# Gated mix of two attentions: maxima from half sums and half differences, branch A in two halves of positions

## The chip, the core and the metric

The kernel runs on one core of a Trainium2 chip. Its time is the device time of one launch in microseconds. Lines are cited as L274, by their number in the kernel's file; the numbers L353 to L508 with a name of the changed kernel beside them are lines of that one.

## The reference

x has 2048 positions of 512 features, everything is fp32, both branches have 32 heads of 16.

```python
g = sigmoid((x * gate_w).sum(-1, keepdims=True))
# A: every position attends to itself and the 7 positions 2, 4, .. 14 before it
qkv = (x @ wqkv) -> q, k, v per head
idx = pos[:, None] - 2 * arange(8)            # masked where < 0
a = softmax(q . k[idx] / 4) @ v[idx] @ wo_A
# B: all heads share one key and one value head, every position sees all 2048
q = (x @ wq) per head;  k = x @ wk;  v = x @ wv    # k, v: 2048 x 16
b = softmax(q k^T / 4) v @ wo_B
out = g * a + (1 - g) * b
```

Branch B alone has 32 x 2048 x 2048 scores. Each is needed twice: once for the row's maximum, once for the exponential.

## The kernel before, in words

Products of full precision are made of three: each operand is split into a rounded part and the rest (`split`; names ending in h and l), and high x high, high x low and low x high are summed.

*Units of branch B.* The queries are cut into 32 units (4 query blocks of 512 x 8 groups of 4 heads). A unit's scores are computed twice. First for the maxima: a "fill" multiplies 128 queries of a unit with 512 keys into PSUM and VectorE reduces it to one maximum per query. A unit has 64 fills, all units 2048; they are taken two at a time into the 1024 wide tile pm (`fill_pair`, L274) or singly into ps or po (`fill_one`, L285). When a unit is complete its maxima are transposed, split (`shift_a`, `shift_c`) and stored by DMA into two more rows of the unit's query tile, so that the second product comes out as score minus maximum. The second time is a "step": 16 steps a unit, 512 in all, each for 128 keys x 2048 query columns. A step is four matmuls (L316) into pe0 and pe1, two exponentials on ScalarE (ACT, L318) into pexp, and four matmuls with the values (`weighted`, L326) that accumulate in po. After a unit's 16th step VectorE transposes po, and GpSimd (POOL) multiplies with the reciprocal of the sum and the gate (L346, L347); every second unit a delayed task transposes the result into ob (`finish_c`).

*Stages.* The prologue makes keys and the first queries. The front runs "lumps" (L698): 14 query lumps (12 matmuls of 128x512; ACT copies, POOL subtracts, SyncE (SP) stores hi, hi, lo) and 64 lumps of branch A's projection (`a_project`, 12 matmuls of 128x384, or 128x402 for the first 16; L159 to L161; ACT copies them to `stage` and every second is stored to the DRAM array ad). The projection's weights come in four groups (`load_wa`, `split_wa`), a group every 16 lumps; the splits and loads are ACT's and POOL's. Between lumps `front_fills` puts fills into pm, pl2, ps and po, as these come free. Then comes the main part: the 512 steps, with the rest of the fills between them (`fill_ready`), and four out phases (`out_phase`, L756), each of which projects four outputs: `prepare` and `turn` put B's and A's result into split form, the matmuls L529 run in 64-row halves on both halves of the PE array, `out_store` adds the halves and stores.

*Branch A* runs on POOL for all 128 partitions, each with 16 consecutive positions, in 16 groups of 2 heads. Per group: `a_load` (L368; one DMA issued by POOL itself: 16 positions and the 14 before them, 96 columns), `a_scores` in two parts (8 products L381, trees of adds L386, L388), VectorE's maximum (`a_max`, L397), POOL's subtraction (L402), ACT's exponential (`a_exp`), VectorE's sum and reciprocal (`a_sum`, L411), POOL's scaling (L418, L419) and `a_values` (8 multiplies L424, 7 adds L426). aext has two buffers, lg, amx and asum two.

*Who sets the order.* Each engine runs its instructions in the order in which the program issues them (manual schedule). The program keeps an estimated clock per engine (`clk`), a time at which each PSUM tile comes free (`free`), a list of `tasks` with due times on PE's clock, and for branch A a clock of POOL (`pool`, ns). `run_pool` issues POOL's next piece of branch A once `pool` is within 3 us of PE's clock, and the other engines' share of a group as a hook with a due time: `a_max` 6000 ns after the scores, `a_exp` and `a_sum` 4000 and 6500 ns after the subtraction. None of these estimates makes an engine wait on the chip; they only fix where in its queue an instruction stands. What an instruction waits for on the chip are its operands and buffers. An out phase starts when branch A has no more pieces to issue, the units of its query block are done and the fills are ahead by less than 1.6 units (`lead`, L753 to L756). In the order that comes out the four out phases stand at steps 320, 369, 417 and 483, and 457 fills are done before the first step, 1591 remain.

Of the kernel before, what the change touches and what calls it, by code (L numbers as in the profile page):

```python
# [6 lines left out]
F32 = mybir.dt.float32  # L7
# [6 lines left out]
P = 128  # L14
# [24 lines left out]
NF = 2 * NU * 2 * 4 * 4  # L39


T_R, T_LAT, T_EXP, T_RED2, T_RED1, T_W, T_LUMP, T_Q = 0.23, 0.20, 0.92, 1.14, 0.61, 1.18, 2.53, 3.2
# [3 lines left out]
def gated_mix_kernel(ctx, tc, xt, wa, wk, wq, wo_a, wo_b, out):  # L46
# [19 lines left out]
    eb = [None, None]  # L66
# [3 lines left out]
    pl = tc.alloc_tile_pool(name="psum_front", bufs=1, space=PSUM)  # L70
    lb = [pl.tile([P, 512], F32, name=f"pl{k}") for k in range(2)]
    eb[1] = pl.tile([P, 2, 512], F32, name="pl2")
# [45 lines left out]
    def load_wa(gg):  # L118
        n = GN + (0 if gg else VN)
        waraw[gg] = p1.tile([P, C, GN + VN], F32, name="waraw", bufs=1)  # L120
        nc.gpsimd.dma_start(waraw[gg][:, :, :n], wa.rearrange("(c p) n -> p c n", p=P)[:, :, GO[gg]:GO[gg] + n])

    def split_wa(gg):
        n = GN + (0 if gg else VN)
        wah[gg] = p1.tile([P, C, GN + VN], F32R, name="wah", bufs=2)
        wal[gg] = p1.tile([P, C, GN + VN], F32R, name="wal", bufs=2)
        split(wah[gg][:, :, :n], wal[gg][:, :, :n], waraw[gg][:, :, :n], nc.gpsimd)
        return 4200
# [25 lines left out]
    nc.vector.tensor_scalar(mk[:, 4:5], mk[:, 5:6], -2.0, 1.0, op0=ALU.mult, op1=ALU.add)  # L154

    def three(out_ap, ah, al, bh, bl):
        mms = []
        for c in range(C):
            mms.append(lambda c=c: nc.tensor.matmul(out_ap, ah(c), bh(c), start=(c == 0), stop=False))  # L159
            mms.append(lambda c=c: nc.tensor.matmul(out_ap, ah(c), bl(c), start=False, stop=False))  # L160
            mms.append(lambda c=c: nc.tensor.matmul(out_ap, al(c), bh(c), start=False, stop=(c == C - 1)))  # L161
        return mms

    def keys(t):
        pk = lb[t % 2]
# [10 lines left out]
    def queries(m, bank):  # L176
        qb, cc = divmod(m, NHG // 2)
        cs = slice(cc * P, (cc + 1) * P)
        mms = three(bank, lambda c: wqh[:, c, cs], lambda c: wql[:, c, cs], lambda c: xh[:, qb, c, :], lambda c: xl[:, qb, c, :])

        def post():
            hi = p0.tile([P, 512], F32R, name="qhi", bufs=3)
            lo = p0.tile([P, 512], F32R, name="qlo", bufs=2)
            if m < 2:
                split(hi, lo, bank)
            else:
                own = p0.tile([P, 512], F32, name="qraw", bufs=1)
                nc.scalar.activation(hi, bank, AF.Copy)
                nc.scalar.activation(own, bank, AF.Copy)
                nc.gpsimd.tensor_sub(lo, own, hi.bitcast(F32))  # L190
            for s, src in enumerate((hi, hi, lo)):
                nc.sync.dma_start(qd[s, :, qb, 8 * cc:8 * cc + 8, :], src.bitcast(F32))

        return mms, post
# [3 lines left out]
    def a_project(gg, j, bank):  # L198
        n = GN + (0 if gg else VN)
        t, r = j // 4, slice(j % 4 * P, (j % 4 + 1) * P)  # L200
        mms = three(bank[:, :n], lambda c: xh[:, t, c, r], lambda c: xl[:, t, c, r], lambda c: wah[gg][:, c, :n], lambda c: wal[gg][:, c, :n])

        def post():
            if j % 2 == 0:
                stage["t"] = p1.tile([P, GC, 2, AN], F32, name="stage", bufs=2)
            nc.scalar.activation(stage["t"][:, :, j % 2, :], bank[:, :GN].rearrange("p (g n) -> p g n", g=GC), AF.Copy)  # L206
            if gg == 0:
                nc.scalar.activation(vst[:, j, 0:DH], bank[:, GN:GN + DH], AF.Copy)
                nc.scalar.activation(gate[:, 1, j:j + 1], bank[:, GN + DH:GN + DH + 1], AF.Copy)
# [628 lines left out]
```

## Time and profile before

| | us |
|---|---|
| median of 3 runs (lowest, highest) | 1558.71 (1558.28, 1558.99) |
| the profiled execution | 1558.82 |
| its span in the trace | 1557.0 |

The table of busy shares in the prediction is over the whole span: an engine at 98% can still be idle where another sets the pace in a short stretch, and an engine at 54% can be full in one stage and idle in the next. So the prediction reads it by stretches of time. The front's query lumps end at 90.1 us, its last projection starts at 311.1, the first weighted product at 315.13; branch A's loads start between 149.2 and 893.0. In a row of groups the columns are line, engine, operation, tile written <- tiles read, shapes, count, then busy us and mean ns, then the idle us of that engine ahead of these instructions and what ended most of it. In a row of the table of stretches they are the stretch, its length, busy us and count of PE, PEld (weight load), VectorE (DVE), ACT, POOL, then granted clock, DMA share and GB/s; where the row is restricted to one line only that line's columns are left. A row of waits names who waited for whom: total us, count, longest us.

### The profile page before, as it was taken

Reading aid. Unit: us, or ns where it says so; the run is one execution under the profiler, and the core shown is the slowest. Engines: PE = TensorE matmul, PEld = TensorE weight load, DVE = VectorE, ACT = ScalarE, POOL = GpSimd, SP = SyncE. Lnnn points to the kernel's source line nnn. Section 1 sums busy time; section 2 is a strip of 40 time slices with the busy share of each in tenths; the row PEclk is TensorE's granted clock in tenths of the full one; section 3 lists DMA queues with packets and bytes.
Section 4 is the critical chain, followed back from the end, with each engine's and each line's share of the span. In section 5 each row is a group of like instructions: output and inputs, shape, how many; then the busy total and the mean of one; then the engine's idle time right before and its main releaser. Section 6 shows DMA issues by size and latency. Waiting matters only on the chain.

```text
span 1557.0 us, 25703 instructions
## 1 busy us (share of the span) xinstructions
PE 1525.7 (98%) x10076; PEld 703.8 (45%) x10076; DVE 1335.8 (86%) x1667; ACT 1120.9 (72%) x1315; POOL 834.2 (54%) x1015
## 2 busy tenths in 40 slices
PE   8999999999999999999999999999999999999998
PEld 4677777733333333333333333363354336333532
DVE  6899999979888898888899889898898889888731
ACT  4223111189999899999989998939966993999676
POOL 7420897778987898889887885240031004000210
PEclk9999999999999999999999999999999999999999
DMA  7842312211011101211111010000000000000000
GB/s 240 261 141 90 120 62 91 99 59 41 21 49 49 56 19 50 65 47 34 50 49 56 20 48 12 22 28 12 12 19 21 12 2 29 2 2 1 2 1 27
DMA packets 42889, 78.61 MB, mean 50 GB/s; under 512 B 8544, under 2 KB 25024, under 8 KB 40720
## 3 DMA queue, kind: packets, MB, share of 16 engines
q1 hardware_dynamic: 20224, 35.56, 7.9%
q0 software_dynamic: 4640, 26.99, 5.0%
q10 hardware_dynamic: 17904, 14.42, 2.8%
q8 instruction: 79, 1.29, 0.3%
q14 instruction: 42, 0.34, 0.1%
HBM read 46.96 MB, written 29.45 MB: 49 GB/s over the span
## 4 chain that ended last, share of the span: by engine, by line
PE 82%; DVE 12%; ACT 4%; issue 1%; DMA 0%; DVEq 0%; POOL 0%; ACTq 0%
PE po L326 30%; PE pe L316 21%; PE pm L253 9%; PE ps L253 8%; DVE mx L274 7%; PE pe L529 5%; DVE mx L285 4%; ACT pexp L318 3%; PE pl L159 3%; PE pl L160 2%; PE pl L161 2%; PE pl L167 1%; PE pl L253 1%; DVE ml L297 0%; PE po L253 0%
## 5 line engine op out<-in xcount | busy, mean ns | idle before, releaser
L318 ACT ACTIVATE pexp<-pe 128x1024 f32<-128x1024 f32 x1022 | 989.2, 1022 | 105.2 <-PE pe L316 100.4
L274 DVE TENSOR_REDUCE mx<-pm 128x2 f32<-128x1024 f32 x610 | 743.9, 1219 | 144.3 <-PE pm L253 140.9
L326 PE MATMUL po<-pexp,vst 128*32 128x512 f32 x4088 | 545.3, 605 | 0.7 <-ACT pexp L318 0.6
L316 PE MATMUL pe<-qst,kst 64*128 64x512 f32 x2044 | 467.0, 452 | 11.1 <-ACT pexp L318 5.8
L316 PEld LDWEIGHTS pe<-qst,kst 64*128 64x128 f32 x2044 | 191.1, 184 | 518.4 <-ACT pexp L318 506.2
L285 DVE TENSOR_REDUCE mx<-ps 128x1 f32<-128x512 f32 x597 | 405.5, 679 | 0.0
L253 PE MATMUL pm<-kst,qst 62*128 62x512 f32 x1230 | 262.6, 417 | 0.8 <-DVE mx L274 0.2
L253 PE MATMUL ps<-kst,qst 62*128 62x512 f32 x597 | 242.6, 406 | 0.4
L381 POOL TENSOR_TENSOR pr<-aext 128x512 f32<-128x512 f32 x128 | 163.9, 1302 | 57.1 <-DMA aext<-ad 57.0
L326 PEld LDWEIGHTS po<-pexp,vst 128*32 128x32 f32 x4088 | 80.4, 108 | 176.4 <-issue 163.3
L206 ACT ACTIVATE stage<-pl 128x384 f32<-128x384 f32 x64 | 31.5, 492 | 165.3 <-PE pl L161 162.8
L426 POOL TENSOR_TENSOR oa<-oa,av 128x512 f32<-128x512 f32 x112 | 143.5, 1281 | 8.8
L346 POOL TENSOR_TENSOR rl<-rl,gate_t 128x16 f32<-128x16 f32 x31 | 6.8, 220 | 242.6 <-DVE rl L342 242.6
L253 PEld LDWEIGHTS pm<-kst,qst 62*128 62x128 f32 x1230 | 117.4, 186 | 41.4 <-DVE mx L274 17.2
L253 PEld LDWEIGHTS ps<-kst,qst 62*128 62x128 f32 x597 | 111.1, 186 | 30.4 <-DVE mx L285 22.3
L424 POOL TENSOR_TENSOR av<-aext,lg 128x512 f32<-128x512 f32 x112 | 118.9, 1061 | 7.5
L305 POOL DMA_DIRECT2D qst<-ml x48 | 27.3, 573 | 134.6 <-DVE ml L297 130.8
L159 PE MATMUL pl<-wah,xh 128*128 128x384 f32 (+1 forms) x256 | 93.7, 366 | 0.4 <-ACT stage L206 0.4
L274 DVE TENSOR_REDUCE mx<-pl 128x2 f32<-128x1024 f32 x75 | 91.1, 1215 | 0.0
L160 PE MATMUL pl<-wal,xh 128*128 128x384 f32 (+1 forms) x256 | 87.1, 340 | 0.0
L161 PE MATMUL pl<-wah,xl 128*128 128x384 f32 (+1 forms) x256 | 86.9, 339 | 0.0
L529 PE MATMUL pe<-woh,turned 64*128 64x512 f32 x496 | 84.3, 400 | 0.1
(124 smaller groups left out, 1204.4 us busy)
## 6 DMA issues: line engine op xcount, KB each, us to landing
aext<-ad POOLq DMA_DIRECT2D x16, 1440.0 KB, 6.2
qst<-qd SPq DMA_DIRECT2D x64, 192.0 KB
ad<-stage ACTq DMA_DIRECT2D x32, 384.0 KB
qd<-qhi SPq DMA_DIRECT2D x32, 256.0 KB
xraw<-xt SPq DMA_DIRECT2D x16, 256.0 KB
qd<-qlo SPq DMA_DIRECT2D x16, 256.0 KB
qst<-ml SPq DMA_DIRECT2D x208, 2.0 KB
out<-two SPq DMA_DIRECT2D x12, 256.0 KB
```

What stands on the lines that cost most here:

```text
L159: mms.append(lambda c=c: nc.tensor.matmul(out_ap, ah(c), bh(c), start=(c == 0), stop=False))
L160: mms.append(lambda c=c: nc.tensor.matmul(out_ap, ah(c), bl(c), start=False, stop=False))
L253: nc.tensor.matmul(dst, qst[v % NB][b:b + 62, pr, t * P:(t + 1) * P], kst[b:b + 62, kc * 512:(kc + 1) * 512], start=True, stop=True)
L274: nc.vector.tensor_reduce(m[:, :, pr, t, kc], dst, AX.X, ALU.max)
L285: nc.vector.tensor_reduce(m[:, odd, pr, t, kc:kc + 1], dst, AX.X, ALU.max)
L316: nc.tensor.matmul(bank[:, odd, :], kst[b:b + 64, kt * P:(kt + 1) * P], qst[u % NB][b:b + 64, pr, :], start=True, stop=True)
L318: nc.scalar.activation(e, bank, AF.Exp, scale=SCALE)
L326: nc.tensor.matmul(po[32 * i:32 * i + 32, :], vst[:, kt, :], pexp[s, i // 2][:, i % 2, :], start=(kt == 0), stop=(kt == NJ - 1))
L381: nc.gpsimd.tensor_mul(pr[:, k], q, e[:, o:o + NJ, AC:2 * AC])
L424: nc.gpsimd.tensor_mul(av, e[:, o:o + NJ, 2 * AC:].rearrange("p j (h d) -> p j h d", d=DH), lg[:, w].unsqueeze(3).to_broadcast([P, NJ, AG, ...
L426: nc.gpsimd.tensor_add(ao, ao, av)
L529: nc.tensor.matmul(eb[x % 2][:, b, :], st[h], mv[h], start=first, stop=last)
```

## The change

*Maxima.* For two keys the larger of two scores s1 and s2 is (s1 + s2)/2 + |s1 - s2|/2. The change computes at the first projection lump (`half_sums`, `half_parts`) half sums and half differences of paired keys, kcd: keys n and n + 512 are a pair. From then on in the front, and where PE's streams of 64-row halves run, an event takes two key blocks of 128 queries at once: `fill_diff` multiplies with the half differences into pm and ACT takes absolute values (L373 of the changed kernel, 2 x 512 wide); `fill_sum` multiplies with the half sums into ps or po, and one VectorE instruction adds the absolute value and reduces with max (L383, tensor_tensor_reduce). Two sums with their event stand for four fills. By the written order 90 events and 180 sums do 360 fills in the front; 451 fills in all are done before the first step, 1597 remain. kcd's tiles take the place of the query tiles; the copies L353 on ACT write them.

*Front in halves.* Each lump's matmuls run as two chains of 64 rows in the two halves of the PE array, beside each other and beside a fill's (`stream`), into the two halves of pe0 or pe1. The two are added after: for query lumps ACT copies, POOL adds, ACT rounds, POOL subtracts; for projection lumps ACT copies one half and VectorE adds (L245). Stores and the rest become tasks.

*Branch A in halves of positions.* Each group's 16 positions are two pieces of 8 (`hf`), first 16 groups for hf = 0, then 16 for hf = 1: 32 loads of 8 + 14 positions (1056 KB in place of 1440), each with its maximum (L499, DVE), subtraction, exponential (L508, ACT), sum and values. `a_scores` makes products of four offsets at a time. `work()` is a generator that yields after each POOL instruction, so that POOL's work stands finer between other things. Hooks are due after 4500, 2500 and 4500 ns. The weight groups are loaded and split in quarters.

*Out phases* may start once the half of branch A that they need is done: they stand at steps 268, 377, 430 and 483; `prepare` and `turn` have single buffers of their own, the next output's come later in the stream, `finish_c` is due after 7 in place of 26 us. `fill_ready`'s slack goes from 0.15 to 0.5 (pm) and 0.3 (ps).

```diff
+NH = NJ // 2
+LEAD, M2S, M1S = 1.5, 0.5, 0.3
...
-    eb = [None, None]
+    eb = [pp.tile([P, 2, 512], F32, name=f"pe{k}") for k in range(2)]
     m2 = pp.tile([P, 2, 512], F32, name="pm")
     m1 = pp.tile([P, 512], F32, name="ps")
     po = pp.tile([P, 512], F32, name="po")
 
...
+    def load_wa(gg, c):
...
+    sel = p0.tile([P, 2, P], F32R, name="sel")
+    for x in range(2):
+        nc.vector.tensor_scalar(sel[:, x].rearrange("p (b s d) -> p b s d", b=2, s=4), whole_k.unsqueeze(2).to_broadcast([P, 2, 4, DH]), 0.5 - x, 0.0, op0=ALU.mult, op1=ALU.add)
...
+    def queries_post(m, bank):
+
+        nonlocal pool
+        settle("rest", 0)
+        two = p0.tile([P, 2, 512], F32, name="two", tag="wqr", bufs=1)
+        nc.scalar.activation(two, bank, AF.Copy)
+        at = after("act", clk["pe"] + T_LAT, 0.92)
+        own = p0.tile([P, 512], F32, name="qraw", bufs=1)
+        nc.gpsimd.tensor_add(own, two[:, 0], two[:, 1])
+        pool = max(pool, 1e3 * at) + 1400
+        hi, lo = parts_of()
+
+        def rest():
+            nonlocal pool
+            nc.scalar.activation(hi, own, AF.Copy)
+            nc.gpsimd.tensor_sub(lo, own, hi.bitcast(F32))
+            pool = max(pool, 1e3 * after("act", 0, 0.6)) + 1400
+            queries_out(m, hi, lo)
...
+
+        tasks.append((pool / 1e3, rest, (), "rest"))
 
     stage = {}
...
+            settle("store", 1)
+            stage["t"] = p1.tile([P, GC, 2, AN], F32, name="stage", bufs=2)
+        st = stage["t"]
+        two = pm[0].tile([P, GN + VN], F32, name="two", bufs=1)
+        nc.scalar.activation(two[:, :n], bank[:, 1, :n], AF.Copy)
+        at = after("act", clk["pe"] + T_LAT, 0.45) + 0.1
+        free[f"e{x}"] = at + 1.5
+
+        def rest():
+            nc.vector.tensor_add(st[:, :, j % 2, :], bank[:, 0, :GN].rearrange("p (g n) -> p g n", g=GC), two[:, :GN].rearrange("p (g n) -> p g n", g=GC))
             if gg == 0:
+                nc.vector.tensor_add(vst[:, j, 0:DH], bank[:, 0, GN:GN + DH], two[:, GN:GN + DH])
+                nc.vector.tensor_add(gate[:, 1, j:j + 1], bank[:, 0, GN + DH:GN + DH + 1], two[:, GN + DH:GN + DH + 1])
+            free[f"e{x}"] = after("dve", at, 0.5 if gg else 0.75) + 0.1
             if j % 2 == 1:
                 dst = ad[gg * GC:(gg + 1) * GC, HALO:, :].rearrange("g (p j) n -> p g (j n)", j=NJ)
+                tasks.append((free[f"e{x}"], lambda: nc.scalar.dma_start(dst[:, :, (j - 1) * AN:(j + 1) * AN], st.rearrange("p g j n -> p g (j n)")), (), "store"))
+            if j == NJ - 1:
+                tasks.append((free[f"e{x}"] + 0.5, whole, (gg,)))
+
...
-    slots = [(v, pr, t, kc) for kc in range(4) for v in range(2) for pr in range(2) for t in range(4)]
+    slots = [(v, pr, t, kc) for kc in range(2) for v in range(2) for pr in range(2) for t in range(4)]
+    slots += [(v, pr, t, kc) for v in range(2) for pr in range(2) for t in range(4) for kc in range(2, 4)]
     slots += [(v, pr, t, kc) for v in range(2, NU) for pr in range(2) for t in range(4) for kc in range(4)]
...
+            if v <= NB:
+                nc.scalar.activation(mx[v].rearrange("p b i t k -> p (b i t k)"), ident[:, 0:64], AF.Identity, scale=0.0, bias=mk[:, 6:7])
...
+    def half_sums():
+
+        clk["pe"] = max(clk["pe"], free["m2"], free["m1"], free["po"]) + 2.0
+        for g in range(2):
+            for x in range(2):
+                for y in range(2):
+                    nc.tensor.matmul(hb[g][x], sel[:, x * y], kst[:, (2 * g + y) * 512:(2 * g + y + 1) * 512], start=(y == 0), stop=(y == 1))
+
+    def half_parts():
+        kcd.append(pm[0].tile([P, 2, 2, 512], F32R, name="kcd", bufs=1))
+        dd.append(pm[0].tile([P, 2, 512], F32, name="dd", bufs=1))
+        for g in range(2):
+            for x in range(2):
+                parts, src = kcd[0][:, g, x], hb[g][x]
+                nc.scalar.activation(parts, src, AF.Identity, scale=mk[:, 0:1])
+                nc.vector.scalar_tensor_tensor(parts, src, mk[:, 1:2], parts.bitcast(F32), op0=ALU.mult, op1=ALU.add)
...
+    def half_mm(dst, v, pr, t, kc, x, odd):
+        b = 64 * odd
+        nc.tensor.matmul(dst, qst[v % NB][b:b + 62, pr, t * P:(t + 1) * P], kcd[0][b:b + 62, kc // 2, x, :], start=True, stop=True)
+
+    def fill_diff():
+        v, pr, t, kc = slots.pop(0)
+        slots.pop(0)
+        for odd in range(2):
+            half_mm(m2[:, odd, :], v, pr, t, kc, 1, odd)
+        at = after("pe", 0, T_R) + T_LAT
+        for odd in range(2):
+            nc.scalar.activation(dd[0][:, odd], m2[:, odd, :], AF.Abs)
+            ready_d[odd] = after("act", at, 0.52) + 0.1
+        free["m2"] = ready_d[1]
+        pend.extend([(v, pr, t, kc, 0), (v, pr, t, kc, 1)])
+
+    def fill_sum():
+        v, pr, t, kc, odd = pend.pop(0)
+        m = unit_tile(v)
+        dst, key = ((m1, "m1"), (po, "po"))[odd]
+        half_mm(dst, v, pr, t, kc, 0, odd)
+        nc.vector.tensor_tensor_reduce(dd[0][:, odd], dst, dd[0][:, odd], 1.0, -FMAX, ALU.add, ALU.max, m[:, odd, pr, t, kc:kc + 1])
+        free[key] = after("dve", max(clk["pe"] + T_R + T_LAT, ready_d[odd]), T_TTR) + 0.08
...
-                tasks.append((at + (26.0 if pieces else 2.0), finish_c, (u, obp["t"])))
+                tasks.append((at + (7.0 if pieces else 2.0), finish_c, (u, obp["t"])))
...
-        t = wp.tile([P, HALO + NJ, AN], F32, name="aext", bufs=2)
+    def a_load(g, hf):
+        e = wp.tile([P, HALO + NH, AN], F32, name="aext", bufs=2)
         src = ad[g]
-        nc.gpsimd.dma_start(t.rearrange("p r n -> p (r n)"), bass.AP(tensor=src.tensor, offset=src.offset, ap=[[NJ * AN, P], [1, (HALO + NJ) * AN]]))
-        aext[g] = t
-
+        nc.gpsimd.dma_start(e.rearrange("p r n -> p (r n)"), bass.AP(tensor=src.tensor, offset=src.offset + NH * hf * AN, ap=[[NJ * AN, P], [1, (HALO + NH) * AN]]))
+        aext[g] = e
+
+    def a_scores(g, hf):
...
+        for w4 in range(0, W, 4):
+            pr = p2[0].tile([P, 4, NH, AC], F32, name="pr", bufs=1)
+            for k in range(4):
+                o = HALO - DIL * (w4 + k)
+                nc.gpsimd.tensor_mul(pr[:, k], q, e[:, o:o + NH, AC:2 * AC])
+                yield 700
...
+                nx = p2[0].tile([P, 4 * NH * AG, n], F32, name=f"tr{n}", bufs=1)
                 nc.gpsimd.tensor_add(nx, cur[:, :, 0:n], cur[:, :, n:2 * n])
+                yield 160 * n + 100
                 cur = nx
-            nc.gpsimd.tensor_add(lg[:, w2:w2 + 2].rearrange("p k j h -> p (k j h)"), cur[:, :, 0], cur[:, :, 1])
-        if half:
-            for w in range(1, W):
...
+    def a_values(g, hf):
...
+            av = p2[0].tile([P, NH, AG, DH], F32, name="av", bufs=1) if w else ao
+            nc.gpsimd.tensor_mul(av, e[:, o:o + NH, 2 * AC:].rearrange("p j (h d) -> p j h d", d=DH), lg[:, w].unsqueeze(3).to_broadcast([P, NH, AG, DH]))
+            yield 700
             if w:
                 nc.gpsimd.tensor_add(ao, ao, av)
-
...
     def prepare(j, n):
-        turned[j] = wp.tile([P, 2, 2, C, P], F32R, name="turned", tag="aext", bufs=2)
+        hi, lo = turned[j, 1] = [pe[0].tile([P, C, P], F32R, name=f"own{x}", bufs=1) for x in range(2)]
...
     def turn(j, n, k):
...
+        hi = pe[0].tile([P, C, P], F32R, name="turned0", bufs=1)
...
+    def stream(seq, mm, done, pooled):
+
+        at, told = [0, 0], 0
+        while min(at) < len(seq):
+            single, odd = None, -1
+            if pend:
+                if free[("m1", "po")[pend[0][4]]] <= clk["pe"] + 0.1 and ready_d[pend[0][4]] <= clk["pe"] + 0.4:
+                    single, odd = fill_sum, pend[0][4]
+            elif paired() and not half:
+                pass
+            elif fillable() and free["m1"] <= clk["pe"] + 0.1:
+                single, odd = lambda: fill_one(m1, "m1"), half[0][4] if half else 0
...
+            dur = 0.0
+            for b in (0, 1) if odd != 1 else (1, 0):
+                if b == odd:
+                    now = clk["pe"]
+                    single()
+                    clk["pe"] = now
+                elif at[b] < len(seq):
+                    dur = mm(b, seq[at[b]])
+                    at[b] += 1
+            after("pe", 0, dur or T_R)
+            if paired():
+                if not half and not pend and max(free["m2"], clk["dve"] - 0.7) <= clk["pe"] + 0.1:
+                    fill_diff()
+            elif slots and fillable() and free["m2"] <= clk["pe"] + 0.1:
+                clk["pe"] = max(clk["pe"], free["m2"])
+                fill_pair(m2, "m2")
+            while told < min(at):
+                told += 1
+                done(seq[told - 1])
...
+    def work():
+
+        def sub(g, hf):
+            yield lambda: ("max", g, hf) in done
+            a_sub(g)
+            hooks.append((pool + 2500, a_exp, g, ("exp", g, hf)))
+            hooks.append((pool + 4500, a_sum, g, ("sum", g, hf)))
+            yield 450
+
+        def values(g, hf):
+            yield lambda: ("sum", g, hf) in done and (g < 8 or p2b)
+            yield from a_values(g, hf)
+            if g == NAG - 1:
+                done.add(hf)
+
+        order = [(g, hf) for hf in range(2) for g in range(NAG)]
+        for i, (g, hf) in enumerate(order):
+            yield lambda: g // GC < ready_gg
+            a_load(g, hf)
+            yield 500 if i else 6000
+            for k, x in enumerate(a_scores(g, hf)):
+                yield x
+                if k == 8 and i:
+                    yield from sub(*order[i - 1])
+            hooks.append((pool + 4500, a_max, g, ("max", g, hf)))
+            if i:
+                yield from values(*order[i - 1])
+            if 0 <= i - 9 < len(wos):
+                yield lambda: p2b
+                for f, a in wos[i - 9]:
+                    f(*a)
+                yield 1300
...
+    pieces, blocked = [work()], []
...
+            if lump[0] == "a" and lump[1:] == (0, 0):
+                settle("rest", 0)
+                half_sums()
+                p0.release()
+                branch_a()
+                pm.append(tc.alloc_tile_pool(name="maxima", bufs=1, side="right"))
+                half_parts()
+            settle(f"post{x % 2}", 0)
+            items[x] = queries(lump[1]) if lump[0] == "q" else a_project(*lump[1:])
+            clk["pe"] = max(clk["pe"], free[f"e{x % 2}"])
+        n = 512 if lump[0] == "q" else GN + (0 if lump[1] else VN)
+        l, r = items[x][i]
+        h = slice(64 * b, 64 * b + 64)
+        nc.tensor.matmul(eb[x % 2][:, b, :n], l[h], r[h], start=(i == 0), stop=(i == 3 * C - 1))
+        return T_R if n == 512 else 0.18
+
+    def done_mm(at):
+        nonlocal pool
+        x, i = at
...
+        k, n = outs // 4, C - (outs >= NJ - 4)
+        if outs < NJ and outs // NH in done and (NHG * (k + 1) - 1 in shaped if n == C else s >= 16 * (NU - 2) + 4) and (lead < LEAD or s >= 16 * (NHG * (k + 2) + 1) - 3):
+            out_phase(list(range(outs, outs + 4)), n)
+            outs += 4
...
-                fill_ready("m2", 0.15)
+                fill_ready("m2", M2S)
             elif which == "m1":
                 ahead = 2 * (16 * (NU - 2) - 8 - s) + 11 * (NJ - 4 - outs)
                 if ahead < to_go() - NF // NU or s >= 16 * (NU - 2) - 8 and ahead + 64 < to_go():
-                    fill_ready("m1", 0.15)
+                    fill_ready("m1", M1S)
```

428 lines of the change are left out of this document (204 added, 224 removed).

## The prediction

> **What bounds the kernel now.** I read the page's busy shares first, then the table of stages, the waits, and last one engine in order of time. The shares, then two stretches (PE, PEld, DVE, ACT, POOL busy; one in the front, one in the main part):
>
> ```profile
> PE 1525.7 (98%) x10076; PEld 703.8 (45%) x10076; DVE 1335.8 (86%) x1667; ACT 1120.9 (72%) x1315; POOL 834.2 (54%) x1015
> 230.00:280.00 50.00, 49.74 (x256) 38.55 (x256) 49.83 (x65) 7.95 (x17) 40.84 (x51) 1.00 0.28 91
> 700.00:800.00 100.00, 99.75 (x688) 35.66 (x686) 89.20 (x109) 90.41 (x98) 84.81 (x106) 1.00 0.15 48
> ```
>
> In the front PE and VectorE (DVE) are both full while ACT idles: the maxima are the price. In the main part PE is full, and ACT, DVE and POOL are all at 85 to 90 in 100. POOL's share over the whole span, 54%, hides that: branch A runs only from about 150 to 980 us, and there POOL has no room. Rows of branch A's load (first and last start), of who waits for it, and of POOL around one load:
>
> ```profile
> L368 POOL DMA_DIRECT2D aext<-ad x16: 549/594/607, 149.2 to 893.0; - x16
> aext<-ad POOLq DMA_DIRECT2D x16, 1440.0 KB, 6.2
> POOL pr L381 <- DMA aext<-ad: 57.0, 12, 6.9
> 434.48 0.59 POOL L368 DMA_DIRECT2D aext<-ad  x1
> 440.81 1.29 POOL L381 TENSOR_TENSOR pr<-aext 128x512 f32<-128x512 f32 x1 [5.73 <-DMA aext<-ad]
> ```
>
> The loads follow each other every (893.0 - 149.2) / 15 = 49.6 us. POOL issues one and its next instruction needs the data, so it stands for 5.73 us. POOL's instructions come in groups (count | busy, mean ns | idle before):
>
> ```profile
> L381 POOL TENSOR_TENSOR pr<-aext 128x512 f32<-128x512 f32 x128 | 163.9, 1302 | 57.1 <-DMA aext<-ad 57.0
> L386 POOL TENSOR_TENSOR tr<-pr 128x512 f32<-128x512 f32 x64 | 81.6, 1276 | 5.0
> L386 POOL TENSOR_TENSOR tr<-tr 128x256 f32<-128x256 f32 x64 | 46.8, 731 | 5.0
> L386 POOL TENSOR_TENSOR tr<-tr 128x128 f32<-128x128 f32 x64 | 25.6, 400 | 5.0
> L388 POOL TENSOR_TENSOR lg<-tr 128x64 f32<-128x64 f32 x64 | 18.8, 293 | 5.0
> L402 POOL TENSOR_TENSOR lg<-lg,amx 128x256 f32<-128x256 f32 x16 | 11.7, 734 | 0.0
> L418 POOL TENSOR_TENSOR asum<-asum,gate 128x32 f32<-128x32 f32 x16 | 3.9, 244 | 12.0 <-DVE asum L412 12.0
> L419 POOL TENSOR_TENSOR lg<-lg,asum 128x256 f32<-128x256 f32 x16 | 11.8, 734 | 1.3
> L424 POOL TENSOR_TENSOR av<-aext,lg 128x512 f32<-128x512 f32 x112 | 118.9, 1061 | 7.5
> L426 POOL TENSOR_TENSOR oa<-oa,av 128x512 f32<-128x512 f32 x112 | 143.5, 1281 | 8.8
> L346 POOL TENSOR_TENSOR rl<-rl,gate_t 128x16 f32<-128x16 f32 x31 | 6.8, 220 | 242.6 <-DVE rl L342 242.6
> L347 POOL TENSOR_TENSOR obp<-tt,rl 128x256 f32<-128x256 f32 x31 | 19.3, 622 | 2.4
> ```
>
> One head group costs POOL 8 x 1.302 + 4 x (1.276 + 0.731 + 0.400 + 0.293) + 0.734 + 0.244 + 0.734 + 8 x 1.061 + 7 x 1.281 = 40.4 us, with 2.3 us of the small idle times, some 0.3 of memsets, and 6.3 for the load: 49.3. L346 and L347 add 0.84 per unit of 16 steps. PE's own pace is read from the exponentials, two a step:
>
> ```profile
> 687.00:987.00 300.00, 266.87 (x276) 1.00 0.13 41
> 315.13 1.06 PE L326 MATMUL po<-early,vst 128*32 128x512 f32 x8
> 1044.79 1.07 PE L326 MATMUL po<-pexp,vst 128*32 128x512 f32 x8
> ```
>
> (The first is L318 alone in that stretch.) 300 / 138 = 2.174 us a step. The order written out puts the maxima of successive head groups (L397, on DVE) 23.6 steps apart, 51.3 us. POOL needs 49.3 + 1.2 = 50.5. So POOL just keeps up, by under 1 us a group; that margin is what the change spends.
>
> **The change, part by part.** *Branch A in halves.* Each half loads 1056 KB in place of 1440, then does 8 products of 256 elements, two trees as long as now (four offsets of half the rows), 8 multiplies and 7 adds of 256. A halved row isn't half a price: 1276 to 731 ns saves 545, not 638. So a product costs 1.302 - 0.545 = 0.757, an add 0.736, a multiply 0.622 (L347 is one, by a broadcast factor), L402 and L419 0.40 each. Busy: 6.06 + 5.40 + 0.40 + 0.24 + 0.40 + 4.98 + 5.15 = 22.6; idle times 1.7, memsets 0.2, less 0.2 where products overlap: 24.3. The load's landing has no row at this size; the nearest:
>
> ```profile
> waraw<-wa POOLq DMA_DIRECT2D x3, 768.0 KB, 4.9
> ```
>
> Bounds 4.5 (6.2 by bytes) and 6.2 (no gain); between the two rows by bytes it is 5.46, but the 768 KB rows are cut finer, so 5.2. The load still stands directly ahead of the product that needs it, 32 times now. Half a group: 24.3 + 5.2 = 29.5 us, two of them 59.0 against 49.3. With L346 and L347 for 12.5 steps 0.66: 30.2.
>
> In the changed order the maxima of successive halves (L499, DVE, behind POOL's last L487) stand 12 to 13 steps apart, at steps 15, 27, 39 ... 265: 250 steps for 20 halves, 12.5 x 2.174 = 27.2 us. POOL is 3.0 us late per half, and 1.3 more in eight that split a weight. DVE then stands at L499; behind it in DVE's queue are the reductions that free pm and ps, PE can't fill those, and behind PE's fill wait the exponentials. ACT's L508 waits for POOL's subtraction likewise. The planner's slack (2.5 to 4.5 us) is spent in two halves; from there POOL sets the pace. The condition is exact: step 317 comes behind the 32nd L499.
>
> When is that? The first load waits for the 16th a-lump's store, so about 149 us as now: what 16 quicker lumps gain, the switch ahead of them costs (below). Then 32 x (landing 5.2 + scores 12.3) + 31 x 0.4 + 30 x 11.8 = 926. Other POOL work queued between, with its rows:
>
> ```profile
> L76 POOL TENSOR_TENSOR wol<-os,woh 128x512 fp32r<-128x512 f32 x8 | 10.2, 1273 | 31.8 <-ACT woh L75 31.8
> L479 POOL TENSOR_TENSOR turned<-own,turned 128x512 fp32r<-128x512 f32 x12 | 15.5, 1294 | 4.8 <-ACT own L478 4.8
> L121 POOL DMA_DIRECT2D waraw<-wa x4 | 3.2, 792 | 0.9 <-POOL wal L76 0.9
> ```
>
> Eight wol 10.2; three such 1.29 for each of the four outputs of the first out phase, now at step 268: 15.5; eight weight loads and splits of 384, 8 x (0.79 + 1.0) = 14.4; L346 and L347 19 times, 16. Sum 56. So 149 + 926 + 56 = 1131 us.
>
> *What is left at step 317.* 616 maxima and three out phases. The old kernel has 613 and three at its step 320, 1044.79: 1557.0 - 1044.8 + 3 x 2.174 = 518.7 us. Span 1131 + 518.7 = 1649.7; the profiled execution adds 1558.8 - 1557.0 = 1.8, and stands 0.1 from the median 1558.71. Forecast **1651 us**.
>
> *The front* is then hidden, but sets the rival. Rows of its lumps, of the out phase, of DVE and ACT, and of the query stretch:
>
> ```profile
> L159 PE MATMUL pl<-wah,xh x256: 332/340/455, 90.1 to 311.1; 128*128 128x384 f32 x96, 128*128 128x402 f32 x32
> 202.07 0.34 PE L159 MATMUL pl<-wah,xh 128*128 128x384 f32 x1
> 202.60 0.34 PE L159 MATMUL pl<-wah,xh 128*128 128x384 f32 x1
> 1011.08 0.49 PE L529 MATMUL pe<-woh,turned 64*128 64x512 f32 x1
> 1028.30 1.10 PE L529 MATMUL pe<-wol,turned 64*128 64x512 f32 x8
> L274 DVE TENSOR_REDUCE mx<-pm 128x2 f32<-128x1024 f32 x610 | 743.9, 1219 | 144.3 <-PE pm L253 140.9
> L285 DVE TENSOR_REDUCE mx<-ps 128x1 f32<-128x512 f32 x597 | 405.5, 679 | 0.0
> L806 DVE TENSOR_TENSOR osl<-pe,part 128x512 f32<-128x512 f32 x4 | 2.6, 686 | 0.7 <-PE pe L802 0.6
> L266 DVE STREAM_TRANSPOSE mt<-ms 128x32 f32<-128x32 f32 x32 | 6.8, 212 | 1.1
> L189 ACT ACTIVATE qraw<-pl 128x512 f32<-128x512 f32 x14 | 8.3, 594 | 5.5 <-POOL qlo L190 5.5
> L497 ACT ACTIVATE two<-pe 128x1024 f32<-128x1024 f32 x16 | 16.4, 1026 | 60.1 <-PE pe L529 60.1
> L171 ACT ACTIVATE kst<-pl,mk 128x512 fp32r<-128x512 f32 x4 | 3.1, 778 | 5.7 <-PE pl L167 5.7
> 30.00:80.00 50.00, 46.10 (x207) 31.85 (x206) 42.79 (x48) 16.26 (x28) 25.60 (x19) 0.97 0.81 240
> ```
>
> Now (311.1 - 90.1) / 63.75 = 3.47 us a lump (the last L159 starts three quarters into it), with 5.9 maxima by the order: DVE 2 x 1.219 + 2 x 0.679 = 3.8, the bound. After: 180 sums (L383) do 360 maxima, each 0.69 (L806 reads PSUM and SBUF as it does) and the reading of the accumulator, 0 to 0.21 (L266, DVE's smallest); I take 0.05, since it is one element. 180 absolute values on ACT, 0.594 each, 107 us, lie beside idle ACT. The adds of two half products (L245) are 64 x some 0.54 on DVE, in place of ACT's copies. PE: 12 rounds a lump as now, 0.177 each at 384 (three in 202.60 - 202.07), 136 in all; per four maxima one round of 0.23 (four in 1.10 with the tail) and two shared with a lump's other half, 0.29: 90 x 0.52 = 47. So PE 183 against 222.
>
> *The switch* is a new wait: kcd lies where the query tiles lay, so ACT's L353 waits for the last query lump's copy (as L497, 1.0), POOL's add 1.3, copy 0.6, split 1.3 and the landing of its store (an estimate, 2 to 6); then four parts as L171, 0.78. Behind L353 in ACT's queue are the copies that free pe0 and pe1, and PE has only the half sums and two lumps until then: 0 to 12 us idle, I take 8. Net gain 30, 10 to 45: the main part starts at 90 + 8 + 183 + 4 = 285 in place of 315.
>
> *Edits at nothing:* the query copies now go through POOL (14 x 1.3 more, in a stretch where it is 25.60 of 50 us busy); ad's store stands in ACT's queue behind L245, but is issued a lump later; the single buffers of the out phase and the planner's wider slack (0.5, 0.3) can cost PE 5 us each way, and POOL covers them; cover gone, they are the +-15 of the first rival. The main part's maxima stay: 1597 against 1591.
>
> The Trainium skill, "SBUF — State Buffer", section "The DMA setup-cost knee", says every transfer pays about 2 us that doesn't shrink with its bytes, fitted as 2 us + bytes / 436 GB/s, and advises one large transfer over several small. For 1056 KB that is an estimate of 4.5 us, and for 1440 KB 5.4 where the trace has 6.2; with 4.5 the forecast would be 22 us less, 1629.
>
> **The rivals.** *POOL isn't the pace (faster).* If the loads were hidden, a half would cost 24.3 + 0.6 + 0.7 = 25.6, under 27.2, and only the front counts: 285 + 317 x 2.174 + 35 for the out phase (now 1011.08 to 1044.79) + 518.7 + 1.8 = 1530. It decides at a landing below 1.4 us. Against: each of the 16 loads now is followed at once by its reader, and so is each of the 32. *POOL nearly keeps up.* Were halves exactly half (0.651, 0.531, 0.640) and the landing 4.5: 26.7 a half, the last L499 at 1041, 1562. Against: the 256- and 512-wide rows of L386. *The maxima don't pay.* With 0.9 a sum DVE takes 90 x (1.8 + 0.55) = 211 us in the front against PE's 183; with the first rival that gives 1558, under the forecast it is hidden.
>
> **How the numbers follow.** POOL's pace 0.80, between 1590 and 1691 (landing 6.2); nearly keeping up, 1545 to 1590, 0.09; only the front, 1515 to 1545, 0.08; slower still, where stalls of PE and POOL add, 0.03. The range 1570 to 1695 leaves out 0.18. About 0.2% (1555.6 to 1561.8) is what can be told from no change: faster 0.10, same 0.02, slower 0.88.
>
> **What would show it.** Right: waits of pr for aext near 32 x 4.6 = 147 us, loads 31 us apart and the last near 1113; DVE's L499 and ACT's L508 waiting for POOL, together near 120 us; POOL near 950 busy; out phase at step 268 near 990 us. Halves near 24.3 + 5.2 prove the sizes. Wrong: L499 without idle time, pr waiting under 2 us a load, or the first step of the main part past 320.

## The result and the profile after

The changed kernel takes 1691.95 us (median of 4 runs, 1691.37 to 1692.53) against 1558.52 us (1558.28 to 1558.99): 1.0856 times as long, 95% interval 1.0837 to 1.0875. The forecast was 1651, its range 1570 to 1695. The span of the profiled execution is 1689.6 us, 132.6 more than before. First the page's shares, then one stretch of the table of stages (PE, PEld, DVE, ACT, POOL busy, then the granted clock):

```profile
PE 1546.6 (92%) x11020; PEld 738.3 (44%) x11020; DVE 1289.7 (76%) x1950; ACT 1227.1 (73%) x1504; POOL 931.4 (55%) x1525
700.00:800.00 100.00, 90.41 (x596) 31.96 (x600) 78.08 (x100) 79.30 (x87) 78.84 (x135) 0.95 0.14 46
```

In the main part no engine is busy throughout any more: PE has fallen from 99.75 to 90.41 in that stretch, and POOL, which was to be the pace, is busy for 78.84. But POOL has no time left all the same. It stands another 14.7 us there for its own three loads, and the rest are gaps between its instructions, 0.08 us each on average; in that stretch it waits for no other engine. From its first load to its last, 978 us, it waits for other engines for 19 us. So POOL and its loads do set the pace, and the others wait for it. The waits (the second row is POOL's in the stretch from 700 to 800 us, the others are of the whole span), and the first and last starts of branch A's loads, of its maxima, and of the first step:

```profile
POOL pr L478 <- DMA aext<-ad: 159.8, 32, 6.5
POOL pr L478 <- DMA aext<-ad: 14.7, 3, 5.1
ACT lg L508 <- POOL lg L504: 96.6, 30, 5.9
DVE asum L513 <- ACT lg L508: 39.3, 23, 5.2
L467 POOL DMA_DIRECT2D aext<-ad x32: 553/593/593, 157.8 to 1135.9; - x32
L499 DVE TENSOR_REDUCE amx<-lg x32: 290/366/380, 185.3 to 1159.0; 128x16 f32<-128x128 f32 x32
L424 PE MATMUL po<-early,vst x8: 1061/1061/1061, 319.7 to 320.5; 128*32 128x512 f32 x8
```

One such wait, in order of time, POOL first, then ACT:

```profile
653.24 0.59 POOL L467 DMA_DIRECT2D aext<-ad  x1
659.12 2.85 POOL L478 TENSOR_TENSOR pr<-aext 128x256 f32<-128x256 f32 x4 [5.29 <-DMA aext<-ad]
665.61 0.46 POOL L504 TENSOR_TENSOR lg<-lg,amx 128x128 f32<-128x128 f32 x1
666.03 1.41 POOL L478 TENSOR_TENSOR pr<-aext 128x256 f32<-128x256 f32 x2
```

```profile
660.17 1.94 ACT L416 ACTIVATE pexp<-pe 128x1024 f32<-128x1024 f32 x2 [0.19 <-PE pe L414]
666.10 0.31 ACT L508 ACTIVATE lg<-lg 128x128 f32<-128x128 f32 x1 [4.00 <-POOL lg L504]
666.32 3.89 ACT L416 ACTIVATE pexp<-pe 128x1024 f32<-128x1024 f32 x4
672.20 1.94 ACT L416 ACTIVATE pexp<-pe 128x1024 f32<-128x1024 f32 x2 [1.99 <-PE pe L414]
```

POOL stands 5.29 us for the load, then does 6.5 us of scores before the subtraction L504. ACT had reached its exponential of branch A (L508) at 662.1 and waits 4.00 us for that subtraction; the step's own exponentials stand behind it in ACT's queue, and behind them PE. That happens at nearly every half.

From the starts of the first weighted product of each step the difference of 132.6 us can be split by where the time appears (rounding leaves 0.1):

| | before | after | difference |
|---|---|---|---|
| first step starts | 315.1 | 319.7 | +4.5 |
| the first three steps | 9.5 | 11.7 | +2.2 |
| 23 steps of more than 4 us, 5.8 us on average (before, 23 mean steps) | 49.4 | 133.4 | +84.0 |
| the other 481 steps, each | 2.149 | 2.204 | +26.3 |
| the four steps with an out phase | 137.3 | 152.8 | +15.5 |
| from the last step to the end | 12.0 | 12.0 | 0 |

The long steps are 12 to 13 steps apart, as the halves' hooks are.

### The profile page after: what moved, and what is told of

It reads as the page before. It is cut to its first block, busy times and chain, and to the rows that moved or that the text cites. A ratio compares the mean times of both kernels' runs of the same rounds, so it can differ in the third digit from the quotient of the medians.

```text
span 1689.6 us, 28993 instructions
## 1 busy us (share of the span) xinstructions
PE 1546.6 (92%) x11020; PEld 738.3 (44%) x11020; DVE 1289.7 (76%) x1950; ACT 1227.1 (73%) x1504; POOL 931.4 (55%) x1525
## 4 chain that ended last, share of the span: by engine, by line
PE 40%; POOL 36%; DMA 12%; ACT 5%; issue 4%; DVE 3%; SPq 0%; POOLq 0%; DVEq 0%; ACTq 0%
PE po L424 13%; DMA aext<-ad 10%; PE pe L414 10%; POOL pr L478 9%; POOL tr L484 7%; POOL oa L531 7%; POOL av L528 6%; PE pe L680 4%; PE pm L299 4%; ACT pexp L416 4%; PE ps L299 3%; PE pe L870 3%; DVE mx L320 1%; DMA qd<-qlo 1%; POOL lg L487 1%
## 5 line engine op out<-in xcount | busy, mean ns | idle before, releaser
L416 ACT ACTIVATE pexp<-pe 128x1024 f32<-128x1024 f32 x1022 | 987.2, 1022 | 134.0 <-PE pe L414 129.4
L320 DVE TENSOR_REDUCE mx<-pm 128x2 f32<-128x1024 f32 x554 | 676.5, 1221 | 208.9 <-PE pm L299 202.9
L478 POOL TENSOR_TENSOR pr<-aext 128x256 f32<-128x256 f32 x256 | 182.1, 734 | 159.9 <-DMA aext<-ad 159.8
L531 POOL TENSOR_TENSOR oa<-oa,av 128x256 f32<-128x256 f32 x224 | 164.3, 734 | 16.8
L528 POOL TENSOR_TENSOR av<-aext,lg 128x256 f32<-128x256 f32 x224 | 139.6, 623 | 14.7
L373 ACT ACTIVATE dd<-pm 128x512 f32<-128x512 f32 x180 | 98.0, 596 | 43.1 <-PE pm L364 38.9
L870 PE MATMUL pe<-wah,xh 64*128 64x384 f32 (+1 forms) x512 | 119.9, 355 | 8.3 <-DVE stage L245 6.1
L870 PE MATMUL pe<-wal,xh 64*128 64x384 f32 (+1 forms) x512 | 120.5, 348 | 0.0
L870 PE MATMUL pe<-wah,xl 64*128 64x384 f32 (+1 forms) x512 | 119.7, 346 | 0.0
L383 DVE CUSTOM_DVE_ANT_0 dd<-ps,dd 128x512 f32<-128x512 f32 x90 | 62.0, 689 | 41.9 <-PE ps L364 19.2
L484 POOL TENSOR_TENSOR tr<-pr 128x512 f32<-128x512 f32 x64 | 81.5, 1273 | 4.8
L870 PEld LDWEIGHTS pe<-wah,xh 64*128 64x128 f32 x512 | 74.7, 194 | 13.7 <-ACT dd L373 6.2
```

The costliest lines, as they stand in the source:

```text
L320: nc.vector.tensor_reduce(m[:, :, pr, t, kc], dst, AX.X, ALU.max)
L373: nc.scalar.activation(dd[0][:, odd], m2[:, odd, :], AF.Abs)
L416: nc.scalar.activation(e, bank, AF.Exp, scale=SCALE)
L478: nc.gpsimd.tensor_mul(pr[:, k], q, e[:, o:o + NH, AC:2 * AC])
L484: nc.gpsimd.tensor_add(nx, cur[:, :, 0:n], cur[:, :, n:2 * n])
L528: nc.gpsimd.tensor_mul(av, e[:, o:o + NH, 2 * AC:].rearrange("p j (h d) -> p j h d", d=DH), lg[:, w].unsqueeze(3).to_broadcast([P, NH, AG, ...
```

## The experiments

**Is it the pace of POOL, or the place that the plan gives to the others?** `work()` yields 500 ns for each load but the first, whose landing it counts (6000). Added up, the plan gives a half 24.2 us, which puts successive halves 12 to 13 steps apart, some 27 us on the chip; there a half took 31.55 us ((1135.9 - 157.8) / 31). The old plan nearly fitted: 48.8 us a group (500 + 2 x 12500 + 800 + 22500) against 49.6. So the first experiment changes this number and leaves POOL's instructions as they are:

```diff
-            yield 500 if i else 6000
+            yield 6000
```

> The changed kernel; only the planner's clock of POOL now counts 6000 ns for every load of branch A, where it counted 500 for all but the first. POOL's instructions are the same; the other engines' share of a half (L499, L508, L513) moves later in their queues, 15 to 16 steps apart in place of 12 to 13. Theory A (a half costs POOL about 30 us with its load, and ACT and VectorE were made to stand behind it): POOL still takes about 30 us a half, but nobody waits for it, so L508's wait for POOL goes from 96.6 us to under 20, steps run at 2.17 us, and the time is about 1555 us (1545 to 1580). Rival B (the new order of the front and of the out phases costs the time, POOL's lateness only follows PE): within 20 us of 1692. Rival C (TensorE's lower granted clock, 0.957, is a cause by itself): the clock stays near 0.95 and the time above 1640.

1550.63 us (1548.39 to 1551.1): 0.9949 of the kernel before, 0.9934 to 0.9964. Its waits, the starts of its loads and of the first step, and the same stretch of its stages:

```profile
POOL pr L478 <- DMA aext<-ad: 135.4, 28, 7.3
L467 POOL DMA_DIRECT2D aext<-ad x32: 551/591/593, 157.6 to 1209.1; - x32
L424 PE MATMUL po<-early,vst x8: 957/1014/1062, 299.0 to 299.9; 128*32 128x512 f32 x8
700.00:800.00 100.00, 100.00 (x700) 36.03 (x697) 90.83 (x119) 91.98 (x101) 73.19 (x123) 1.00 0.16 49
```

POOL still waits 135.4 us for its loads, and it now takes longer over branch A: the last load starts at 1209.1 in place of 1135.9. Yet the kernel is 141 us shorter, because ACT waits no more for POOL's subtraction (L508 waits once, for 0.3 us, in place of 96.6 us), PE is full, and no step after the third lasts over 4 us but those with an out phase. POOL's slowness alone is not the cost. Its slowness with ACT's and VectorE's instructions placed for a faster POOL is. The front gains too: the first step starts at 299.0, so in the changed kernel some 21 us of the front's gain were lost to the same waits (18 of them in four lumps, of 9.4, 8.1, 5.0 and 6.9 us among lumps of 2.9).

**The same from the other side, in the kernel before.** Nothing of the change, one number of the plan:

```diff
-    QK, AV = 12500, 22500
+    QK, AV = 10000, 22500
```

> The kernel before with one number changed: QK, the plan's time for half a group's scores, 10000 in place of 12500 ns, so that the plan leaves out about 5 us a group, as the changed kernel's plan does with a half's landing. POOL's instructions stay as they are. Theory A (it is the plan that ties the other engines to POOL): the maxima of successive groups stand 21.3 steps apart in place of 23.6, the 16th at step 251, where the kernel before is at 860 us and POOL's 16th group has its scores near 925: some 65 us slower, 1623 us (1600 to 1645), with ACT's exponential of branch A waiting for POOL's subtraction. Rival (the order alone is harmless): 1550 to 1570.

1621.74 us (2 runs, 1619.59 and 1623.89), 1.0409 of the kernel before (1.0387 to 1.0431). Its loads and the new wait:

```profile
L368 POOL DMA_DIRECT2D aext<-ad x16: 547/592/604, 149.4 to 890.6; - x16
ACT lg L406 <- POOL lg L402: 57.4, 15, 8.0
```

POOL does its 16 loads in the time that it took before (149.2 to 893.0 there) and gains nothing from being asked earlier; the others lose 63 us. A plan that is too short by 5 us a group is enough for that, with no halves at all.

**Hiding the landing.** Here the plan stays too short, and POOL becomes quicker: from the main part on a third buffer for aext, and the next half's load ahead of this half's values.

```diff
+        if len(early) % 3 == 2:
+            e = p2b[0].tile([P, HALO + NH, AN], F32, name="ahalf", bufs=1)
...
             hooks.append((pool + 4500, a_max, g, ("max", g, hf)))
+            if i + 1 < len(order) and p2b:
+                a_load(*order[i + 1])
+                yield 500
             if i:
                 yield from values(*order[i - 1])
```

> The changed kernel; from the main part on branch A has a third load buffer, and the next half's load is issued ahead of this half's values, some 12 us before its reader; the plan's due times stay as they are (tt and the tail's tile share other buffers to make room; the front's loads stay as they were). Theory A: the wait of pr for aext falls from 159.8 us to about 32 (the front's six loads), a half costs POOL about 25.6 us, under PE's 27; the main part starts near 320 as it did and then runs at its own pace: about 1575 us (1560 to 1605). Rival B (as for the run before): within 20 us of 1692. Rival D (landing isn't the price, since the halves' instructions alone are too many for POOL): 1640 or more with the wait for aext gone.

1578.76 us (1577.97 to 1582.75), 1.0131 (1.0114 to 1.0148).

```profile
POOL pr L483 <- DMA aext<-ad: 32.7, 6, 6.0
ACT lg L513 <- POOL lg L509: 17.7, 5, 6.2
700.00:800.00 100.00, 99.69 (x700) 36.00 (x697) 89.33 (x121) 91.26 (x100) 89.73 (x154) 1.00 0.17 56
```

Of 159.8 us the wait for loads keeps the front's six, ACT's wait for POOL keeps four in the front and one, and the main part is as full as before the change. So a half without its landing fits the 12 to 13 steps that the plan leaves it, though barely (POOL is busy for 89.73 of 100 us), and the landing is what made the plan too short. The first step is at 320.5 as in the changed kernel: the front, where the loads were left as they were, doesn't gain.

**Branch A's halves alone**, in the kernel before, with the changed kernel's plan for them; front, maxima and out phases as before; `a_load` to `a_values` and `work()` are those of the change's diff:

```diff
-    pieces = [("load", 0)]
...
-        pieces += [("qk0", g)] + ([("sub", g - 1)] if g else []) + [("qk1", g)] + ([("val", g - 1)] if g else [])
+    pieces, blocked = [work()], []
```

> The kernel before with branch A alone changed: 32 half pieces with the changed kernel's pieces, due times and plan; front, maxima and out phases as before. Theory A: loads 30 to 31 us apart, the 32nd maximum (step 345) near 1120 us, L508's counterpart waits for POOL by some 100 us in all, the time 1620 us (1590 to 1650). Rival F (halves are harmless without the new front): 1555 to 1575.

1676.62 us (2 runs, 1675.35 and 1677.9), 1.076 (1.0739 to 1.0782): 57 us more than expected.

```profile
L369 POOL DMA_DIRECT2D aext<-ad x32: 547/594/607, 147.3 to 1144.4; - x32
ACT lg L410 <- POOL lg L406: 76.0, 27, 4.7
POOL asum L423 <- DVE asum L416: 36.3, 4, 13.4
230.00:280.00 50.00, 50.00 (x257) 38.56 (x257) 49.79 (x67) 8.04 (x18) 24.94 (x54) 1.00 0.23 78
```

Halves with the short plan give most of the loss by themselves. The loads stand 32.2 us apart on average, not 30 to 31, and the reason lies in the front: the first five gaps between loads are 37.3 us on average, the other 26 are 31.2. In the front POOL waits for VectorE's sums (the row with L416, taken from 147 to 335 us), and VectorE is full there with the maxima (49.79 of 50 us). The expectation had left that out. Besides, one step (343) took 14.6 us; why was not looked for.

**The front and the maxima alone**: branch A in 16 whole groups in the changed kernel, with the old due times.

```diff
-NH = NJ // 2
+NH = NJ
...
-        order = [(g, hf) for hf in range(2) for g in range(NAG)]
+        order = [(g, hf) for hf in range(1) for g in range(NAG)]
```

> The changed kernel with branch A in 16 whole groups again (NH = NJ, two offsets at a time, due times of the kernel before, a third ob buffer, two of the out phase's tiles in aext's place): front in halves and maxima from half sums alone. Theory A: 16 loads and about 50 us a group again, the first step of the main part at 300 to 312 us in place of 315, the time about 1550 us (1535 to 1570). Rival B: within 20 us of 1692. Rival E (the front doesn't gain by itself): first step at 318 or later, time 1560 or more.

1564.59 us (1562.11 to 1567.46), 1.004 (1.0027 to 1.0054). In that kernel the values of one projection lump for the last eight heads were overwritten; it was run again with one line that adds them up in time:

> As e3_whole_groups, with one line more: the last projection lump's predecessor is added up before its PSUM tile is taken for the first step (there one lump's values of the last eight heads were overwritten; the instructions are the same in number). Its time should be that of e3_whole_groups, 1564 us (1560 to 1568), with the first step near 304. Were the front alone worth what theory A said, 1550.

1564.55 us (1563.45 to 1566.86), 1.0039 (1.0025 to 1.0053). Rival E's time, but not for its reason: the first step is at 304.8, 10 us earlier than before. The gain is given back in the main part. The out phases take 36.46, 36.46, 36.47 and 39.05 us against 35.70, 35.37, 35.72 and 30.49: 11.2 us more; the first three steps take 4.4 more; the others 2.155 against 2.149, 3 more. So the out phases, which I had costed at nothing, are a third part of the change, and a loss.

**The switch to half sums.** In the run with the landing counted PE stands idle for 11.65 us at the first projection lumps. ACT's first kcd copy in that run:

```profile
97.19 0.69 ACT L353 ACTIVATE kcd<-pm,mk 128x512 fp32r<-128x512 f32 x1 [6.89 <-DMA qd<-qlo]
```

kcd lies where qhi and qlo lay, so it waits until the last query store has landed. The front's right-hand pool is split in two, so that kcd lies over the weights wqh and wql:

```diff
+    pa = tc.alloc_tile_pool(name="phase0a", bufs=1, side="right")
     p0 = tc.alloc_tile_pool(name="phase0", bufs=1, side="right")
...
-        return p0.tile([P, 512], F32R, name="qhi", bufs=3), p0.tile([P, 512], F32R, name="qlo", bufs=2)
+        return pa.tile([P, 512], F32R, name="qhi", bufs=3), pa.tile([P, 512], F32R, name="qlo", bufs=2)
```

> The kernel with the landing counted in the plan; besides, the tiles of kcd lie over wqh and wql and no longer over qhi and qlo (the front's right-hand pool is split in two), so that L353 doesn't wait for the last query lump's store. Theory A's term for the switch (the wait for the store's landing stands on PE's path, 6.9 us there): L353's wait for the DMA of qlo is gone, the lump with the switch takes about 10 us in place of 16.7, the first step comes near 292 in place of 299.0 and the time is 1544 us (1541 to 1548). Rival G (behind it VectorE or POOL is late by as much): no change, 1549 to 1552.

1543.84 us (1541.75 to 1545.61), 0.9908 (0.9893 to 0.9923), and the first step at 290.8. The same copy there, behind ACT's work and no DMA:

```profile
89.76 0.67 ACT L354 ACTIVATE kcd<-pm,mk 128x512 fp32r<-128x512 f32 x1
```

**The out phase's buffers.** In the runs above PE waits for the subtraction that `turn` now leaves until the output before is stored, as its buffer turned1 is single. Of the last out phase of the run with the landing counted:

```profile
1451.75 0.50 PE L680 MATMUL pe<-woh,own 64*128 64x512 f32 x2 [1.57 <-DVE turned L596]
```

```diff
-            lo = pe[0].tile([P, C, P], F32R, name="turned1", bufs=1)
+            lo = pe[0].tile([P, C, P], F32R, name="turned1", bufs=2)
...
-        later[j] = rest
+        rest()
```

> As the run e5_switch_early, and turned1 of the out phase has two buffers, so that its subtraction is issued right behind its copies and not after the output before is stored. In the run with the landing counted the last out phase took 39.0 us between two steps against 30.5 in the kernel before, with PE waiting 1.6 us for VectorE's L596 three times, and the others 36.4 to 36.6 against 35.4 to 35.7. Theory (the single buffers cost that): the last out phase near 33 us, the others 35.5, 8 us less than e5_switch_early: 1536 us (1531 to 1541). Rival: buffers hidden, within 2 us of it.

1537.73 us (1536.35 to 1538.35), 0.9868 (0.9854 to 0.9883): 6 us, not 8. The last out phase falls from 39.02 to 31.45 (in the executions profiled, where the first step stands 2.1 us later); those before stay at 36.5, and their extra 1 us each is something else, which wasn't looked for. This version, the change with the landing in its plan, kcd moved and turned1 doubled, takes 1.3% less than the kernel before.

## Why the prediction was right, point by point

*The mechanism* held: loads stand directly ahead of their readers 32 times (159.8 us of waits against the 147 forecast), 31.55 us apart (31), and the others stall until branch A is through. The first out phase begins near 992 us (990), and POOL is busy for 931.4 us (950). The first rival's time (POOL not the pace) is nearly what hiding the landing or planning for it gives, once the front is taken off that is later than its 285: 1578.76 less 35.5 and 1550.63 less 14.0, so 1543 and 1537, against 1530. That rival's "landing below 1.4 us" does not come out of its own terms, which give 27.2 - 24.3 - 0.7 = 2.2 us; no run tests either figure.

*The number* was held narrowly. 1691.95 lies 3 us inside the range and 1 us above the 1590 to 1691 that the prediction gave to POOL's pace, whose upper end was meant for a landing of 6.2 us. The landing was shorter than that; terms that the sum had at nothing or too small, below, filled the difference. That the time stayed inside the range is in part luck.

*But POOL's pace alone decides nothing.* The prediction compared POOL's 30.2 us with PE's 27.2 between two maxima, and took the 12 to 13 steps between them as given. They are a choice of the plan, and the runs with that number changed, in either kernel, show that it matters as much: at 15 to 16 steps POOL may be as slow as it is. The step "POOL sets the pace" should read "the order makes the others keep a pace that POOL can't".

*Where the stall stands.* "DVE then stands at L499" was wrong: the view of that line has no idle time ahead of it, which the prediction itself had named as a sign of being wrong. ACT's L508 does, 96.6 us, and DVE's L513 behind it, 39.3; together 136 against 120 forecast for both. L508 is due 2500 ns after POOL's subtraction, which stands behind the first part of the next half's scores and so behind the next load; L499, due 4500 ns after the scores, has no load between.

*Sizes of a half.* Groups of POOL, after:

```profile
L478 POOL TENSOR_TENSOR pr<-aext 128x256 f32<-128x256 f32 x256 | 182.1, 734 | 159.9 <-DMA aext<-ad 159.8
L531 POOL TENSOR_TENSOR oa<-oa,av 128x256 f32<-128x256 f32 x224 | 164.3, 734 | 16.8
L528 POOL TENSOR_TENSOR av<-aext,lg 128x256 f32<-128x256 f32 x224 | 139.6, 623 | 14.7
aext<-ad POOLq DMA_DIRECT2D x32, 1056.0 KB, 5.4
```

734, 734 and 623 ns against 757, 736 and 622; the busy time of a half comes out at 22.5 us as forecast (22.6). The landing took 5.4 us, of which POOL stood 5.0, plus 0.59 for issuing: 5.6 against 5.2. The Trainium skill, "SBUF — State Buffer", "The DMA setup-cost knee", gives 4.5 us by its fit, an estimate that the trace doesn't bear out; with it the forecast would have been 1629, further off.

*The 41 us that were missing.* Up to step 317, 1159.8 against 1131: 8.8 for the first load (157.8, not 149; the switch cost more than the front had gained by then), 13 for the landings (32 times 0.4), 15 for POOL's own waits for VectorE's reciprocals, which the sum had at nothing, less 8 that were not traced to a term. Those waits, from the first load to the last:

```profile
L444 POOL TENSOR_TENSOR rl<-rl,gate_t 128x16 f32<-128x16 f32 x19 | 4.2, 224 | 15.0 <-DVE rl L440 15.0
```

After it 529.8 against 518.7: the three out phases take 112.1 us where the kernel before has 101.6. The term that failed there was "the single buffers of the out phase ... POOL covers them": behind the last load nothing covers them. Of these 10.5 us the last out phase has 7.2 (37.68 against 30.49), about what doubling turned1 gave back in its run; the other two have 1.7 each, whose cause stays open.

*The front* was forecast at 285 and hidden. Hidden it was, but it stands at 319.7 by POOL's waits, 299.0 without them, 290.8 without the switch's store. The switch cost about 12 us (a lump of 14.7 in place of 2.9; 16.7 in the run with the landing counted), where I took 8 from 0 to 12. Its estimate of 2 to 6 us for the landing of the query tile's store was not measured by itself; in the run with the landing counted ACT's wait for that store is 6.89 us, and without it the first step comes 8.2 us earlier. Sums and lumps were sized rightly: 0.69 us and 0.08 for the accumulator against 0.69 + 0.05, and lumps of 2.91 (mean of 53, without the long ones) against 183 / 64 = 2.86.

## What to carry to other kernels

Where an order is written by a plan, a change of one engine's work isn't finished before the plan's durations are measured again: a term too short by 5 us in 30 cost 9% here, while counting it in full cost nothing though the slow engine then finished later, since nobody needed its result soon. Compare planned with measured time per piece first, before making the slow engine faster. An instruction that must wait for a slow engine belongs late in a busy engine's queue, because everything behind it waits as well.

## What the hardware showed besides

After a stall PE runs slowly for a while. Five stretches of 5 us around the stall shown above, and one cut to fit the slow time (PE, PEld, DVE, ACT, POOL, then the granted clock):

```profile
655.00:660.00 5.00, 5.00 (x38) 1.82 (x34) 4.38 (x6) 4.58 (x5) 0.88 (x2) 1.00 0.67 253
660.00:665.00 5.00, 3.90 (x30) 1.23 (x26) 3.67 (x5) 1.94 (x2) 4.69 (x8) 1.00 0.00 0
665.00:670.00 5.00, 2.62 (x11) 1.20 (x15) 1.98 (x4) 3.87 (x5) 4.84 (x7) 0.66 0.00 0
670.00:675.00 5.00, 5.00 (x29) 1.92 (x22) 2.28 (x3) 2.22 (x4) 4.39 (x13) 0.66 0.00 0
675.00:680.00 5.00, 5.00 (x39) 1.78 (x39) 4.56 (x6) 4.58 (x5) 4.53 (x7) 1.00 0.30 81
666.60:673.40 6.80, 6.02 (x26) 2.45 (x30) 3.12 (x5) 4.78 (x6) 6.23 (x14) 0.50 0.00 0
```

Some 3.5 us pass without a matmul, and the clock is at 0.66 on average for 10 us: at half for 6.8 us. The step right after a long one takes 3.15 us (mean of 23), the second 2.26, the next ones 2.13 to 2.24. That is most of the 26.3 us of the ordinary steps in the table, about 1 us a stall, and it goes with the span's clock of 0.957. The Trainium skill, "TensorE: Matmul & The Clock Gate", Part 1, says that the array falls to half its clock after an idle window of about 3.4 us and returns after a busy one of that length. The trace agrees in the half, and the times are near: the clock falls some 2.7 us into a gap of 3.47 us and is back 6.8 us later. The clock did not start the loss: with the landing counted it is 0.989 and the slow steps are gone. Whether PE at full clock would have shortened the changed kernel, or only waited longer for POOL, was not tried.
